# First expert's rows, w2 and the stores re-ordered at the handover from a recurrence to a mixture of experts

## Chip, cores and metric

One core of a Trainium2 chip runs the whole kernel as one launch. The metric is device microseconds. The time before is the median of three runs, 1148.8 us (1147.38 to 1150.54).

## What is computed

A gated linear recurrence over 4 sequences of 5056 steps and 256 channels, then a mixture of 8 experts over all 20224 rows, each row with one expert. Routing is greedy over the sorted logits, with a capacity of 2528 rows for each expert:

```python
f = lower_bound + (1 - lower_bound) * sigmoid(f_logit)
for t in range(S):
    h = f[:, t] * h + (1 - f[:, t]) * x[:, t]
    y[:, t] = h
logits = y.reshape(N, D) @ w_gate
# in descending order of all logits: token -> expert, unless taken or full
for e in range(E):
    hid = maximum(x[mask_e] @ w1[e], 0)
    out[mask_e] = hid @ w2[e]
```

## The kernel before, in words

**Stage one** goes over 40 chunks of four 128-row tiles (the last has two). For chunk i, `load` (L171) brings `f_logit` and `x` with two SyncE transfers, three chunks ahead, into pool `pin` (names `fl`, `xl`, four buffers each). `sig` (L843) is ScalarE's sigmoid and a product, on GpSimd for most chunks. `fwd` (L866) transposes both on TensorE (`pf`, `pb`), ScalarE makes the factor `fg`, VectorE scans to `g`. `back` (L896) multiplies `g` by identity and gate weights in fp32 (`iw`), which turns it back and adds the logits (`pr`, four PSUM buffers); ScalarE and VectorE copy this to `hr`, one slot of a ring of 22, and `store` (L921) writes it to `hbuf` in DRAM (528 KB). SyncE takes loads and stores in program order. The loop at L982 writes all this out by hand: iteration i does `fwd(i)`, `sig(i + 2)` and `back(i - 1)`; how many stores have been made by then is set by `SR` at L1010, and their order is `TURN` (L919).

**Beside stage one** a first, provisional expert is prepared from the first 72 tiles (18 chunks, `CE`): `prep` finds each row's best expert, `early` (L728) chooses the expert with the fewest rows above 896 and lists these rows, in jobs that ride along in `back`'s PSUM buffers. `first_weights(0..2)` (L964) bring its w1 in two halves of 0.5 MB and its w2 of 1 MB by indirect GpSimd transfers; `first_rows(q)` (L973) gathers its first four tiles of rows from `hbuf`, which needs the first 18 chunks stored. `low_half` (L978) makes the low parts of w1 (products are made of a high and a low fp32r part: `xh`, `xl`, `hh`, `hl`, `w1h`, `w1l`, and `w2s` with both).

**The handover** is at L1134: the remaining stores are issued, the stage-one pools are closed, and the pools of `moe` (L1146) are laid over the ring, so that the first writes into `hh`, `w2s` and others wait for the stores of the chunks that lay there.

**The experts**: slot -1 is the provisional expert's first 15 tiles, then come the slots 0 to 7. `trans` (L1323) turns gathered rows into `xh` and `xl`; `first` (L1342) makes six matmuls of 512 columns into `pw` (three PSUM buffers) for each of 8 blocks j, ScalarE makes `hh` and VectorE `hl` from it; `second` (L1372) multiplies by `w2s`, three steps behind (`LAG`). Everything else goes on between these: `tick` (L1551) gives steps to the routing (`main`), to the lists of rows (`comp`; `further` (L783) for slot -1) and to the split of weights (`sp`, `split`, L1233). Class `Pace` (L23) keeps an account of estimated engine times, and a step is emitted only if its engine is no more than 2 us ahead of TensorE in this account. Gathers of later rows are issued one per step, each held by the latest `hh`.

What stands at the handover in `moe`:

```python
XG[-1, 0] = g["XGE"].rearrange("p (q r) -> p q r", q=4)
asked[-1, 0] = 0
sp = Bg(split(-1))
trans(-1, 0, 0, True)
trans(-1, 0, 1, True)
g["low_half"](1)
for _ in range(2):
    sp.tick(True)
gather(*gathers.pop(0))
```

Of the kernel before, what the change touches and what calls it, by code (L numbers as in the profile page):

```python
# [7 lines left out]
F32 = mybir.dt.float32  # L8
F32R = mybir.dt.float32r
BF = mybir.dt.bfloat16  # L10
# [3 lines left out]
AF = mybir.ActivationFunctionType  # L14
# [92 lines left out]
def kernel(ctx: ExitStack, tc: tile.TileContext, x: bass.AP, f_logit: bass.AP,  # L107
# [9 lines left out]
    P = 128  # L117
# [16 lines left out]
    NX = NT + ND  # L134
    hbuf = dram.tile([N, ROW], F32, name="hbuf")
    ohp = ctx.enter_context(tc.tile_pool(name="ohp", bufs=2))
    ip = ctx.enter_context(tc.tile_pool(name="ip", bufs=E + 1))
# [9 lines left out]
    RING = 22  # L147
    SR = 0.5
    PS, RW, CP = 2, NT - CE, 136
# [4 lines left out]
    pre = ExitStack()  # L154
    pring = pre.enter_context(tc.tile_pool(name="pring", bufs=RING))
    pwork = pre.enter_context(tc.tile_pool(name="pwork", bufs=2))
# [9 lines left out]
    def rows_tile(dt):  # L166
        return pin.tile([P, KT * ROW], dt, name="fl")
# [171 lines left out]
    W = state.tile([P, NC], F32, name="W")  # L339
    MK = state.tile([P, NG, 16, 8], BF, name="MK")  # L340
    K16 = state.tile([P, NC], I16, name="K16")
# [386 lines left out]
    def early(wi, ids):  # L728
# [19 lines left out]
        yield  # L748
        first_weights(2)
        w = CE + 2  # L750
# [32 lines left out]
    def further(rt, ids, prog):  # L783

        cut(0, CE)
        yield 'DVE',
        for _ in prep(CP, NC):
            yield 'DVE',
        prog["all"] = True
        ranks(CE, NT)  # L790
        w = NT - CE + 2
        yield 'PE', RSE, ecnt
        ps = rt.tile([P, 512], F32, name="rt")
        offsets(ps, w)
        yield 'DVE', ps
        st = ohp.tile([P, len(groups)], F32, name="st")
        g1 = {}

        def ge(k):
            g1[k] = ohp.tile([P, 512], BF, name="g1")  # L800
            v.tensor_scalar(g1[k], IO, st[:, k:k + 1], None, op0=OP.is_ge)
        for k in range(2):
            v.tensor_scalar(st[:, k:k + 1], ps[:, 160:161], -512.0 * k, None, op0=OP.add)
        steps_of(ps, w, MORE)
        ge(0)
        at = EARLY // P
        for k, n in enumerate((4, MORE // P - 4)):
            yield 'PE', RAE, g1[k]
            ps = rt.tile([P, 512], F32, name="rt")
            for b in range(n):  # L810
                nc.tensor.matmul(ps[:, b * w:(b + 1) * w], g1[k][:, b * P:(b + 1) * P], RAE[:, :w], start=(b == 0),
                                 stop=(b == n - 1), skip_group_check=True)
            yield 'DVE', ps
            if k == 0:
                ge(1)
            yield from blocks(ps, 4 * k, n, w, CE * P, ids[:, at:at + n], True)
            at += n
            prog["ids"] = at
# [77 lines left out]
    def back(i, job=None):  # L896
        t0, n, _ = chunks[i]
        HR[i] = pring.tile([P, KT, ROW], F32, name="hr")
        for k in range(n):
# [18 lines left out]
    ST = {}  # L918
    TURN = [*range(18), 24, 18, 19, 20, 21, 23, 22, *range(25, NCH)]  # L919

# [47 lines left out]

    WSE, WSL, lows = [], [], []

    XGE = None

# [9 lines left out]
    for i in range(NCH + 1):  # L982
# [5 lines left out]
        if i < NCH:  # L988
            fwd(i)
        if i == NCH - 4:  # L990
            assert stored * KT >= CE
            XGE = rows_tile(F32R)
            first_rows(0)
        if i == 0:
# [3 lines left out]
        if i + 2 < NCH:  # L998
            sig(i + 2)
        if i == NCH - 4:  # L1000
            for q in range(1, KT):
                last_first = first_rows(q)
        if NCH - 2 <= i < NCH:
            WSE.append(pin.tile([P, FB, P], F32R, name="xl"))
            h = i - NCH + 2
            nc.scalar.activation(WSE[h][:, :4], RAWE[0][:, h].rearrange("p (q j) -> p j q", j=FB)[:, :4],
                                 AF.Identity, scale=omlb[:, h:h + 1])
        if i >= 1:
            back(i - 1, job)
            while stored < min(i - 1, int(SR * (i - 1)) + (i > 30)):  # L1010
                store(TURN[stored])
                stored += 1
        if i >= 4:
            build(2)
        if i > NCH - 2:
            h = i - NCH + 1
            WSL.append(pin.tile([P, FB, P], F32R, name="xl"))
            lows.append(h)
        upto = chunks[i - 1][0] // 8 * 8 if i else 0
# [3 lines left out]
        elif CE <= done < CP and upto >= done + 32:  # L1023
            preps.append(prep(done, done + 32))
            done += 32
        prep_step(99 if i == NCH else 3 if done == CE and upto < CE + 8 else PS if done < CE else (i != NCH - 4) + (i > NCH - 3))
        while lows and lows[0] == 0:
            low_half(lows.pop(0))
        if est is None and done >= CE and not preps:
# [89 lines left out]
    def afresh(rt):  # L1119
# [12 lines left out]
        ends(full)  # L1132

    for i in TURN[stored:]:  # L1134
        store(i)
# [10 lines left out]
def moe(ctx, tc, g):  # L1146
# [383 lines left out]
    prog[-1]["ids"] = EARLY // P  # L1530
    XG[-1, 0] = g["XGE"].rearrange("p (q r) -> p q r", q=4)
    asked[-1, 0] = 0
    sp = Bg(split(-1))
    trans(-1, 0, 0, True)
    trans(-1, 0, 1, True)
    g["low_half"](1)
    for _ in range(2):
# [13 lines left out]
    def tick():  # L1551
# [9 lines left out]
        if k < 0 and wn == 0 and sp is not None:  # L1561
            sp.tick(True)
            if sp.done:
# [155 lines left out]
```

## Time and profile before

| | |
|---|---|
| median of 3 runs | 1148.8 us |
| the profiled execution | 1148.47 us |
| its span (first to last instruction) | 1146.7 us |
| mean granted TensorE clock | 0.998 |
| TensorE busy | 1129.9 us, 99% |
| VectorE, ScalarE, GpSimd busy | 764.8, 542.1, 477.6 us |

Times in the rows are microseconds from the span's start. PE is TensorE's matmuls, PEld its weight loads, DVE VectorE, ACT ScalarE, POOL GpSimd, SPq SyncE's queue. Nearly all instructions are recorded through one helper, so they carry its line, L100, and are told apart by their tiles. In a timeline a row may merge several instructions (x4), and the bracket at its end is the idle time before it and what ended it. A matmul's end is modelled, so neighbouring rows overlap a little.

### The profile page before, as it was taken

The numbers are of one execution on the slowest core, as the hardware profiler recorded it, in microseconds if no ns is written. First come the engines' busy times: TensorE is split into PE (matmuls) and PEld (weight loads), VectorE is DVE, ScalarE is ACT, GpSimd is POOL, SyncE is SP. The second block draws the span as 40 slices with busy tenths as digits, with TensorE's granted clock in tenths as the row PEclk, the third lists the DMA queues.
The fourth block names the chain that finished last, engine by engine and source line by source line (L and its number), as shares of the span: only waits on it lengthen the run. The fifth ranks groups of instructions, "written<-read, shape, count | busy, mean of one in ns | idle before, by whom it ended". The sixth has DMA issues, their size and how long they took to land.

```text
span 1146.7 us, 21286 instructions
## 1 busy us (share of the span) xinstructions
PE 1129.9 (99%) x7905; PEld 1008.9 (88%) x7905; DVE 764.8 (67%) x2233; ACT 542.1 (47%) x1141; POOL 477.6 (42%) x486
## 2 busy tenths in 40 slices
PE   9999989999999999999999999999999999999997
PEld 7999879989888888888889888898889888888887
DVE  7999997778777446776875877656444643463342
ACT  7889873263337532643544444345434532242221
POOL 5777642243335663333433433343334333433322
PEclk9999999999999999999999999999999999999999
DMA  9999995131131111311311311131113111321100
GB/s 353 374 355 371 394 341 152 38 112 43 48 111 39 40 52 50 115 48 42 120 47 43 112 47 41 48 115 48 46 43 110 58 42 49 108 62 46 42 32 32
DMA packets 52947, 125.23 MB, mean 109 GB/s; under 512 B 8563, under 2 KB 28789, under 8 KB 51685
## 3 DMA queue, kind: packets, MB, share of 16 engines
q0 software_dynamic: 20016, 61.01, 16.5%
q1 hardware_dynamic: 32544, 62.78, 15.5%
q8 instruction: 64, 1.05, 0.4%
q14 instruction: 47, 0.38, 0.1%
q10 hardware_dynamic: 276, 0.01, 0.0%
HBM read 81.79 MB, written 42.10 MB: 108 GB/s over the span
## 4 chain that ended last, share of the span: by engine, by line
PE 91%; DMA 3%; DVE 2%; issue 1%; ACT 1%; POOL 1%; POOLq 0%; DVEq 0%; ACTq 0%; SPq 0%
PE pw L100 39%; PE py L100 35%; PE rt L100 7%; PE pr L100 5%; PE pb L100 2%; PE pf L100 2%; DVE g L100 1%; PE pt L100 1%; DMA fl<-in_f_logit_dram 1%; DMA hbuf<-hr 1%; DMA r<-in_moe_w_dram,wi 1%; DVE hl L100 0%; ACT fg L100 0%; POOL out_dram L100 0%; ACT hh L100 0%
## 5 line engine op out<-in xcount | busy, mean ns | idle before, releaser
L100 PE MATMUL py<-w2s,hh 128*128 128x256 f32 (+2 forms) x2120 | 434.4, 296 | 0.0
L100 ACT ACTIVATE hh<-pw 128x512 fp32r<-128x512 f32 (+3 forms) x328 | 190.8, 582 | 496.9 <-PE pw L100 439.7
L100 DVE SCALAR_TENSOR_TENSOR hl<-pw,hh 128x512 fp32r<-128x512 f32 (+3 forms) x328 | 219.3, 669 | 214.4 <-ACT hh L100 213.1
L100 PEld LDWEIGHTS py<-w2s,hh 128*128 128x128 f32 (+1 forms) x2120 | 341.9, 188 | 20.8 <-issue 0.2
L100 PE MATMUL py<-w2s,hl 128*128 128x256 f32 x1136 | 319.8, 282 | 0.0
L100 POOL DMA_INDIRECT out_dram<-y,ids x160 | 162.7, 1017 | 304.7 <-ACT hh L100 248.2
L100 POOL DMA_INDIRECT fl<-hbuf,ids x160 | 164.4, 1028 | 267.6 <-ACT hh L100 193.6
L100 PE MATMUL pw<-xh,xl 128*128 128x512 f32 (+3 forms) x672 | 231.6, 387 | 1.2 <-DVE hl L100 0.9
L100 PEld LDWEIGHTS py<-w2s,hl 128*128 128x128 f32 x1136 | 212.8, 187 | 2.0
L100 PEld LDWEIGHTS pw<-xh,xl 128*128 128x128 f32 x672 | 124.8, 189 | 19.5 <-DVE hl L100 1.3
L100 PE MATMUL pw<-xl 128*128 128x512 f32 (+3 forms) x336 | 130.5, 389 | 0.1
L100 PE MATMUL pw<-xl,w1h 128*128 128x512 f32 (+1 forms) x320 | 127.0, 397 | 0.0
L100 PE MATMUL pw<-xh,w1h 128*128 128x512 f32 (+1 forms) x320 | 126.3, 395 | 0.0
L100 PE MATMUL pw<-xh,w1l 128*128 128x512 f32 (+1 forms) x320 | 126.2, 394 | 0.0
L100 POOL TENSOR_TENSOR xl<-fl,xl 128x1024 f32<-128x1024 f32 x37 | 87.7, 2369 | 40.2 <-ACT fl L100 22.0
L100 DVE TENSOR_TENSOR_SCAN g<-fg,g,pb 128x512 f32<-128x512 f32 (+4 forms) x78 | 92.8, 1227 | 6.8 <-ACT fg L100 6.1
L100 PE MATMUL pr<-iw,g 128*128 128x136 f32 x632 | 81.1, 280 | 0.5 <-ACT hr L100 0.5
L100 ACT ACTIVATE junk<-rt,r 128x182 bf16<-128x182 f32 (+2 forms) x153 | 61.4, 402 | 37.3 <-DVE r L100 32.7
L100 PEld LDWEIGHTS pr<-iw,g 128*128 128x128 f32 x632 | 76.4, 190 | 1.0 <-ACT hr L100 0.9
L100 PEld LDWEIGHTS pw<-xh,w1l 128*128 128x128 f32 x320 | 60.2, 188 | 11.3
L100 PEld LDWEIGHTS pw<-xl 128*128 128x128 f32 x336 | 63.7, 190 | 5.9 <-DVE xl L100 0.5
L100 PEld LDWEIGHTS pw<-xh,w1h 128*128 128x128 f32 x320 | 60.4, 189 | 8.0
(271 smaller groups left out, 1537.6 us busy)
## 6 DMA issues: line engine op xcount, KB each, us to landing
hbuf<-hr SPq DMA_DIRECT2D x39, 528.0 KB, 9.9
fl<-in_f_logit_dram SPq DMA_DIRECT2D x38, 512.0 KB, 6.7
xl<-in_x_dram SPq DMA_DIRECT2D x38, 512.0 KB, 7.2
fl<-hbuf,ids POOLq DMA_INDIRECT x160, 2.8
out_dram<-y,ids POOLq DMA_INDIRECT x160, 2.4
fl<-in_f_logit_dram SPq DMA_DIRECT2D x3, 256.0 KB, 4.1
xl<-in_x_dram SPq DMA_DIRECT2D x3, 256.0 KB, 4.5
r<-in_moe_w_dram,wi POOLq DMA_INDIRECT x27, 5.3
```

What stands on the lines that cost most here:

```text
L100: r = f(*args, **kw)
```

## The change

The rows of the first expert are gathered into a buffer that shares its place with the routing masks (`mk`), in iterations 35 to 37 instead of 36. They are turned, in two of stage one's PSUM buffers, ahead of the last `back`, by `turn_first`, in place of the two calls of `trans`. `first_weights(2)` moves from `early` (about iteration 28) to iteration 37. The ring's slots get fixed names, laid out by `PLACE`, so that the pools of `moe` cover other chunks' slots. One store more is made from iteration 9, 17 and 25 on, 18 at most until iteration 37. The low half 0 comes right after `back(38)`, the low half 1 ahead of `back(39)`. In `further` the last `prep` comes ahead of `cut`. Slot -1's split of weights takes a step at every second tick.

```diff
+    mk = ctx.enter_context(tc.tile_pool(name="mk", bufs=1))
-    SR = 0.5
-    pring = pre.enter_context(tc.tile_pool(name="pring", bufs=RING))
+    pring = pre.enter_context(tc.tile_pool(name="pring", bufs=1))
+    PLACE = [2, 3, 4, 7, 8, 9, 6, 5, 18, 19, 20, 21, *range(10, 18), 0, 1]
+    for s in PLACE:
+        pring.tile([P, KT, ROW], F32, name=f"hr{s}")
-    MK = state.tile([P, NG, 16, 8], BF, name="MK")
+    XGE = mk.tile([P, NG * 64], F32R, name="MK")
@@ early
-        first_weights(2)
@@ further
+        for steps in (*preps, prep(CP, NC)):
+            for _ in steps:
+                yield 'DVE',
         cut(0, CE)
         yield 'DVE',
-        for _ in prep(CP, NC):
-            yield 'DVE',
@@ back
-        HR[i] = pring.tile([P, KT, ROW], F32, name="hr")
+        HR[i] = pring.tile([P, KT, ROW], F32, name=f"hr{i % RING}")
-    TURN = [*range(18), 24, 18, 19, 20, 21, 23, 22, *range(25, NCH)]
+    TURN = [*range(18), 18, 22, 19, 23, 20, 21, *range(24, NCH)]
+    MOST = CE // KT
+    def turn_first():
+        xs = [rows_tile(F32R)[:, :1024].rearrange("p (h w) -> p h w", h=2) for _ in range(2)]
+        pts = [ppr.tile([P, 512], F32R, name="pr") for _ in range(2)]
+        for h, pt in enumerate(pts):
+            for q in range(KT):
+                at = q * ROW + h * (P + E)
+                nc.tensor.transpose(pt[:, q * P:(q + 1) * P], XGE[:, at:at + P], ident_r)
+            nc.scalar.activation(xs[0][:, h], pt.bitcast(F32), AF.Copy)
+        for h, pt in enumerate(pts):
+            nc.vector.tensor_tensor(xs[1][:, h], pt.bitcast(F32), xs[0][:, h].bitcast(F32), op=OP.subtract)
+        return xs
@@ the loop over chunks
-        if i == NCH - 4:
-            assert stored * KT >= CE
-            XGE = rows_tile(F32R)
-            first_rows(0)
-        if i == NCH - 4:
-            for q in range(1, KT):
-                last_first = first_rows(q)
+        for q in {NCH - 5: (0,), NCH - 4: (1, 2), NCH - 3: (3,)}.get(i, ()):
+            assert stored >= MOST
+            last_first = first_rows(q)
+        if i == NCH - 3:
+            first_weights(2)
+        if i == NCH:
+            WSL.append(pin.tile([P, FB, P], F32R, name="xl"))
+            XSE = turn_first()
+            low_half(1)
         if i >= 1:
             back(i - 1, job)
-            while stored < min(i - 1, int(SR * (i - 1)) + (i > 30)):
+            while stored < min(i - 1, (i - 1) // 2 + (i > 8) + (i > 16) + (i > 24), MOST if i < NCH - 3 else i):
                 store(TURN[stored])
                 stored += 1
-        if i > NCH - 2:
-            h = i - NCH + 1
+        if i == NCH - 1:
             WSL.append(pin.tile([P, FB, P], F32R, name="xl"))
-            lows.append(h)
+            low_half(0)
-        prep_step(99 if i == NCH else ...)
-        while lows and lows[0] == 0:
-            low_half(lows.pop(0))
+        prep_step(0 if i == NCH else ...)
+    MK = mk.tile([P, NG, 16, 8], BF, name="MK")
@@ moe
-    XG[-1, 0] = g["XGE"].rearrange("p (q r) -> p q r", q=4)
-    asked[-1, 0] = 0
+    XS[-1, 0] = g["XSE"]
     sp = Bg(split(-1))
-    trans(-1, 0, 0, True)
-    trans(-1, 0, 1, True)
-    g["low_half"](1)
@@ tick
         if k < 0 and wn == 0 and sp is not None:
-            sp.tick(True)
+            if count[0] % 2:
+                sp.tick(True)
```

## Rows read from the trace of the kernel before

**Rows 1.** The page's first part, TensorE's entry of it.

```profile
PE 1129.9 (99%) x7905; PEld 1008.9 (88%) x7905; DVE 764.8 (67%) x2233; ACT 542.1 (47%) x1141; POOL 477.6 (42%) x486
```

**Rows 2.** Windows: length, busy us (instructions) by engine, granted clock, DMA share, GB/s.

```profile
20.00:40.00 20.00, 20.00 (x180) 20.00 (x179) 19.51 (x29) 17.98 (x31) 13.98 (x13) 1.00 1.04 393
120.00:140.00 20.00, 18.99 (x160) 17.79 (x160) 18.48 (x29) 17.82 (x35) 15.54 (x12) 1.00 1.05 392
159.00:165.00 6.00, 4.33 (x15) 2.86 (x15) 4.50 (x11) 4.48 (x7) 1.77 (x3) 0.73 1.07 357
165.00:171.00 6.00, 5.12 (x25) 4.02 (x24) 6.00 (x11) 3.46 (x7) 0.00 (x0) 0.98 1.10 341
240.00:400.00 160.00, 160.00 (x1207) 142.60 (x1206) 114.72 (x334) 79.59 (x206) 74.28 (x71) 1.00 0.19 57
```

**Rows 3.** Timeline of TensorE at the handover: start, us, instruction, idle before.

```profile
155.89 3.05 PE L100 MATMUL pr<-iw,g 128*128 128x136 f32 x24
...
160.09 0.28 PE L100 MATMUL pt<-identr,fl 128*128 128x128 f32 x1 [1.03 <-DMA fl<-hbuf,ids]
160.56 0.28 PE L100 MATMUL pt<-identr,fl 128*128 128x128 f32 x1 [0.19 <-DMA fl<-hbuf,ids]
...
161.53 0.61 PE L100 MATMUL pw<-xh,xl 128*128 128x512 f32 x1 [0.34 <-ACT xh L100]
...
168.67 0.50 PE L100 MATMUL pw<-xh,xl 128*128 128x512 f32 x1 [0.89 <-DVE hl L100]
```

**Rows 4.** The chain of waits, a group of six matmuls at full clock.

```profile
250.20 1.38 PE pw L100 x6
```

**Rows 5.** Timeline of VectorE around the handover.

```profile
150.33 1.48 DVE L100 TENSOR_TENSOR xl<-fl,xl 64x1024 f32<-64x1024 f32 x1
...
157.76 0.41 DVE L100 COPY hr<-pr 128x264 f32<-128x264 f32 x1
...
161.51 0.69 DVE L100 TENSOR_TENSOR xl<-pt,xh 128x512 fp32r<-128x512 f32 x1 [1.46 <-ACT xh L100]
...
162.72 1.14 DVE L100 SCALAR_TENSOR_TENSOR xl<-r,omlb,xl 128x512 fp32r<-128x512 f32 x1
...
167.91 0.70 DVE L100 SCALAR_TENSOR_TENSOR hl<-pw,hh 128x512 fp32r<-128x512 f32 x1
```

**Rows 6.** Timeline of GpSimd: the request of w2, then the first expert's gathers.

```profile
109.52 1.01 POOL L100 DMA_INDIRECT r<-in_moe_w_dram,wi  x1 [0.16 <-issue]
...
147.22 1.08 POOL L100 DMA_INDIRECT fl<-hbuf,ids  x1 [2.77 <-DMA hbuf<-hr]
...
150.88 1.85 POOL L100 DMA_INDIRECT fl<-hbuf,ids  x1 [0.16 <-PE pf L100]
...
154.34 0.99 POOL L100 DMA_INDIRECT fl<-hbuf,ids  x1 [0.30 <-issue]
```

**Rows 7.** Landing times: loads of 97 to 99, of 107 to 109, then w2's.

```profile
DMA to landing us min/median/max: 4.6/5.3/5.9
DMA to landing us min/median/max: 11.1/11.3/11.5
DMA to landing us min/median/max: 10.5/10.5/10.5
```

**Rows 8.** Timelines of ScalarE and VectorE behind the late load.

```profile
118.77 1.06 ACT L100 ACTIVATE fl<-fl 128x1024 f32<-128x1024 f32 x1 [2.56 <-DMA fl<-in_f_logit_dram]
121.37 2.45 DVE L100 TENSOR_TENSOR_SCAN g<-fg,g,pb 128x512 f32<-128x512 f32 x2 [1.92 <-ACT fg L100]
```

**Rows 9.** Timeline of SyncE's queue: a pair of stores, and the last stores.

```profile
120.36 1.55 SPq L923 DMA_DIRECT2D hbuf<-hr  x2
...
141.55 36.36 SPq L923 DMA_DIRECT2D hbuf<-hr  x22
```

**Rows 10.** Timelines of GpSimd and TensorE later on: a held gather, a gap.

```profile
186.25 1.02 POOL L100 DMA_INDIRECT fl<-hbuf,ids  x1 [25.47 <-ACT junk L100]
238.34 0.31 PE L100 MATMUL rt<-RA,g 128*128 128x160 bf16 x2 [1.95 <-DVE RA L100]
```

More of the change, by code (lines that the diff above doesn't have):

```diff
@@ L967, in first_weights @@
                                      in_offset=bass.IndirectOffsetOnAxis(ap=WIE[:, n:n + 1], axis=0))
-    WSE, WSL, lows = [], [], []
-    XGE = None
+    WSE, WSL = [], []
+    def turn_first():
[9 more added lines that the diff above has]
+        return xs
     def first_rows(q):
@@ L1025 @@
             done += 32
-        prep_step(99 if i == NCH else 3 if done == CE and upto < CE + 8 else PS if done < CE else (i != NCH - 4) + (i > NCH - 3))
-        while lows and lows[0] == 0:
-            low_half(lows.pop(0))
+        prep_step(0 if i == NCH else 3 if done == CE and upto < CE + 8 else PS if done < CE else (i != NCH - 4) + (i > NCH - 3))
         if est is None and done >= CE and not preps:
```

## Prediction

> **What bounds the kernel.** I read the page's busy shares first, then the windows, then the engines' own timelines around the point where the first stage hands over to the experts. TensorE is busy 1129.9 of 1146.7 us [rows 1], and from 240 us on it has no gap to give: 160.00 of 160.00 us at full clock [rows 2]. The change does not shorten that part, so whatever it wins or loses ahead of 240 us should arrive at the end almost unchanged.
>
> Two places ahead of 240 us hold lost time. One is the handover. The last product of stage one is 24 fp32 matmuls (with the chunk before it) from 155.89 on, 3.05 us, to 158.9. TensorE then waits 1.03 us for the third block of gathered rows, starts the first expert product at 161.53 and its fourth group only at 168.67, after 0.89 us of waiting for `hl` [rows 3]. At full clock a group of six takes 1.38 us [rows 4]; the three groups are 4.1 us, and the eight transposes about 0.5. So 168.67 - 158.9 - 4.6 = **5.2 us** are lost here. Part of it is clock: the mean granted clock of 159 to 165 is 0.73, so the engine ran some of that time on the 1.2 GHz level, after its waits [rows 2]. VectorE is the other half: it stands idle for 1.46 us until 161.51, waiting for the turned rows, and then has no gap (6.00 of 6.00 us from 165 to 171), with the first `hl` only at 167.91 [rows 2, 5].
>
> The other place is the last third of stage one. From 20 to 40 us TensorE loses nothing while 393 GB/s move; from 120 to 140 it runs 160 matmuls instead of 180, which at the earlier rate is 2.2 us lost, and VectorE is busy 18.48 [rows 2]. Loads issued at 97 to 99 us land after 5.3 us (the median of the row); those issued from 107 on, beside the first expert's weights, need 11.1 to 11.5 [rows 6, 7]. ScalarE waits 2.56 us for such a load at 118.77, and VectorE 1.92 us right behind it [rows 8].
>
> **The change part by part.** *Rows earlier.* The first gather stands at 147.22 after 2.77 us of waiting for a store, the fourth at 154.34 [rows 6], and the rows it brings are turned at 160.56, 6.2 us later [rows 3]. In the new order the first 18 chunks are stored by iteration 31 instead of 35, and the gathers are issued one iteration (3.6 us) earlier for the first, with the fourth at iteration 37. By POOL's order I put the fourth at about 151, so by the same 6.2 us, or one more under load, it lands at 157.2 to 158.2, just as the transposes can start (below). The buffer is the mask's; the masks come into use some 15 us after the transposes, so that wait costs nothing.
>
> *Turned ahead of the last product.* The transposes now stand in front of the last eight fp32 matmuls. They need the PSUM buffer that VectorE's copy of the chunk before frees at 158.1 [rows 5]. The two copies of the last chunk move 0.9 us back; the expert product's second PSUM bank waits for one of them. VectorE's idle 1.46 us is filled, and its order becomes: both `xl`, the low half, the last copies, then the product's needs.
>
> *Split at half the rate.* Before, VectorE ran six weight or routing steps ahead of the first `hl`. With one split step in two ticks, one 1.1 us half and one 0.6 us half of the weights move behind it. Today VectorE ends its copies at 160.05; without them, 0.6 us, it is free at 159.5. Counting its steps from there, by their lengths where they stand in [rows 5] and 0.25 us for each small routing step (an estimate from the timeline they fill between those rows): `xl` 1.2, low half 1.1, copies 0.6, three routing steps 0.75, a low half 1.2, another step 0.25, `hl` 0.6: the first `hl` ends near 165.2, and the fourth group can start some 3.4 us sooner than 168.67. But the second product needs the first low half of w2, which now comes behind another 1.2 us half and, if the planner lets the routing go first, 1.1 us of that: 167.2 to 168.3, against 170.2 before (168.67, a group, and the first matmul behind it). So the handover gives **2.0 to 3.0 us**; bounds 0 (rows late) and 3.4. I take 2.5, the middle of the inner pair, as both orders of the routing steps are open.
>
> *Weights for w2 later.* One megabyte leaves 109.52 [rows 6] for iteration 37. At 393 GB/s that is 2.7 us of transfers off the queue ahead of the late load. Against it stand three stores made sooner (1.4 us each at that rate), one of them at iteration 25, just before. So the late load comes 1.3 to 2.7 us sooner and ScalarE's 2.56 us shrink to about 1 or to nothing. TensorE gets back at most the 1.92 us of VectorE's wait, since VectorE is the bound afterwards; bounds 0 and 1.9, I take **1.2**, nearer the upper end because the pair of stores at 120.36 [rows 9], which follows the late load today, is gone as well. In its new place the transfer is queued on POOL for 1.0 us ahead of small copies that nobody needs for 5 us, and it lands beside the stores: issued at about 152, with 10.5 us as measured under load [rows 7], at 163, when ScalarE is ready for it. Cost 0 to 1 us, taken as 0: the slack is VectorE's, which needs its half at 166 or later.
>
> *Stores.* 22 stand behind the last load in both kernels (from 141.55 on [rows 9]). The end of the queue, which releases the third chunk's gather at 186.25 [rows 10], stays within 1 us of where it is: 2.7 us more for w2, less for the calmer queue ahead of it. The gather's product starts some 10 us later, so I cost this at nothing; without that cover it would be up to 3 us. The order of need matters where `hh` and `w2s` overwrite ring slots: those stores are the first six in either order, no wait shows before, and I count none.
>
> *Later.* The 1.95 us gap at 238.34 [rows 10] is caused by ScalarE's wait for the next weights in program order; the change does not touch it. The planner may shift it: 0 in the sum, 1.5 us either way in the range.
>
> **Sum.** Stage one 1.2 and handover 2.5 are 3.7 us. The profiled execution took 1148.47 us (span 1146.7, 1.8 around it), 0.3 under the median of 1148.8: 1148.5 - 3.7 = 1144.8, against the median 1145.1. I say **1145.0**, 0.33% under the median. About 0.3% (3.4 us) is what a measurement of this kernel can tell from no change, so this forecast lies on the edge.
>
> **A rule that speaks against it.** The gather issued at 150.88 took 1.85 us where the one at 154.34 took 0.99; VectorE's 64 x 1024 product of two SBUF tiles, from 150.33 on, ran beside the long one [rows 5, 6]. The fourth gather would move next to that product and could be 0.85 us later, on TensorE's path, since it is due within 1 us of its use; I leave that in the range. The Trainium skill, "SBUF — State Buffer", section "Who interferes with whom", says that a VectorE instruction with two SBUF inputs and a GpSimd instruction reading SBUF exclude each other for the whole instruction; the rows agree for this pair, and by the rule the sum would be 2.9 us rather than 3.7.
>
> On the shared transfers the row is the pair of loads that needed 11.1 to 11.5 us beside the weights [rows 7]. The Trainium skill, "DMA: Bandwidth & Descriptors", section "Issuing engines are not separate DMA queues", says that transfers of all queues run on the same 16 engines and interleave; by it w2 slows the last stores instead of the loads and nothing is saved in total, only placed where less waits.
>
> **The rivals.** *A, as above:* 1145.0, own range 1142.5 to 1146.0, chance 0.5.
> *B, the handover stays bound.* The fourth gather slips one iteration (3.6 us) or VectorE's queue takes the routing steps first. Then the transposes hold up the last product of stage one too, and what is left is VectorE's filled 1.46 us, or stage one's 1.2: 1147.0 to 1147.3. For it speaks that VectorE is the engine without slack on both sides of the handover; against it, that POOL is idle for 25 us later on and has room. It also covers a part that does not do what it says. Chance 0.38.
> *C, the early stores.* Stores doubled at iterations 9, 17 and 25 push loads past their need. A load that lands 2.56 us too late had needed up to 11.5 us, so the limit is about 8.9 [rows 7, 8]; the 20 us that begin with today's doubled store at 120.36 lost 2.2 us [rows 2, 9]. Three such places are 6.6 us; less 2.5 at the handover this gives 1148.5 + 4.1 = 1152.6. It decides from some 3.5 us of added landing time. Against it: a landing of 5.3 us ahead of the third place, and one store adds 1.4. Chance 0.12.
>
> So faster by over 0.3%: 0.5; within: 0.38; slower: 0.12. The range takes in the best case (1.9 + 3.4 = 5.3 us, and some from the gap at 238), and B with the planner's 1.5 us and w2's 1 us on the bad side: 1142 to 1150.5.
>
> **What would show it.** Right: no wait for gathered rows in front of the transposes; first expert matmul near 159.7 and fourth group near 165 to 166 on stage one's old clock; the granted clock of that stretch nearer 1; ScalarE's wait at 118.77 about 1 us or gone; no group of waits for loads near 45, 72 and 100 us. Wrong: a `w2s` or `hl` wait of over 2 us, a wait for the rows, a new wait near 199 us or 238 us that gives the time back.

## The result, and the profile after

The changed kernel is **slower**: 1155.94 us (median of six runs, 1154.61 to 1157.02) against 1150.61 us (1147.38 to 1151.33) for the kernel before, a ratio of 1.0055 (95%: 1.0046 to 1.0065). The forecast was 1145.0, with 1150.5 as the upper end. The profiled execution took 1154.61 us, span 1152.8; that of the kernel before 1148.47, span 1146.7. The 6.1 us between the spans are what has to be explained.

The page's first part, TensorE's and the others' busy time after, answers to [rows 1].

```profile
PE 1130.8 (98%) x7921; PEld 1013.5 (88%) x7921; DVE 763.7 (66%) x2231; ACT 541.7 (47%) x1142; POOL 477.9 (41%) x486
```

No engine has more to do: TensorE 0.9 us more, VectorE 1.1 less. The time is waiting, and the windows say where. After, with the columns of [rows 2] (length, busy us and instructions of PE, PEld, DVE, ACT, POOL, granted clock, DMA share, GB/s):

```profile
120.00:140.00 20.00, 19.39 (x172) 19.17 (x173) 19.47 (x34) 18.54 (x33) 15.51 (x12) 1.00 0.96 355
159.00:165.00 6.00, 5.07 (x24) 3.47 (x22) 5.83 (x13) 3.85 (x9) 2.72 (x3) 1.00 1.05 364
165.00:173.00 8.00, 6.17 (x26) 5.25 (x27) 7.85 (x18) 1.08 (x2) 0.00 (x0) 0.79 1.09 349
240.00:400.00 160.00, 160.00 (x1206) 142.68 (x1206) 113.80 (x330) 78.57 (x202) 75.24 (x72) 1.00 0.19 57
460.00:480.00 20.00, 16.71 (x100) 14.27 (x99) 12.19 (x41) 10.46 (x19) 6.88 (x7) 0.91 0.37 125
```

and two of these stretches in the kernel before:

```profile
165.00:173.00 8.00, 7.12 (x37) 5.57 (x35) 7.97 (x17) 3.46 (x7) 0.00 (x0) 0.99 1.10 340
460.00:480.00 20.00, 19.60 (x134) 17.51 (x133) 16.00 (x52) 12.90 (x24) 8.58 (x9) 1.00 0.42 138
```

The first two lines are what the prediction spoke of, and they gain. From 120 to 140 us TensorE runs 172 matmuls instead of 160. From 159 to 165 it is busy 5.07 us at clock 1.00, where it was busy 4.33 at 0.73. The third line gives that back (below). The last is a stretch the prediction never looked at: 2.9 us of busy time are missing there, and the clock is 0.91.

A way to see when a lead is lost is the start of ScalarE's k-th `hh` in its timeline, less the start of the same one in the profile of before (negative: ahead; us):

| | 1st (165) | 5th (173) | 9th (187) | 25th (237) | 29th (249) | 93rd (450) | 101st (475) | last (1137) |
|---|---|---|---|---|---|---|---|---|
| after | -3.31 | +0.09 | +0.06 | +0.14 | +1.72 | +1.36 | +5.83 | +6.14 |
| after, on a second chip | -4.06 | -0.66 | -0.68 | -0.34 | +1.17 | +0.85 | +3.53 | +3.52 |
| before, again | +0.37 | +0.29 | +0.26 | +0.51 | +0.42 | +0.53 | +0.60 | +0.61 |
| stores alone (below) | -1.07 | -1.13 | -1.13 | -0.94 | +0.45 | +0.39 | +0.51 | +0.52 |
| old list (below) | -2.48 | -1.37 | -0.05 | -0.04 | +1.42 | +1.43 | +1.81 | +1.87 |
| six memsets (below) | -3.58 | -0.15 | -0.19 | +2.06 | +4.05 | +3.72 | +3.75 | +3.97 |
| hold (below) | -3.38 | +0.01 | -0.04 | -2.73 | -2.07 | -1.66 | -2.34 | -2.92 |
| hold on before | +1.95 | +1.82 | +1.81 | -0.66 | +0.13 | -0.06 | -0.72 | -1.27 |

(Single executions, on three chips. Where the routing's matmuls fall between the products shifts a value too: the 23rd of after stands at +4.42, between +0.55 at the 21st and +0.14 at the 25th.) So three things happen: 3.3 us won are gone eight us later; 1.6 us go between 237 and 249 (0.8 of it is TensorE's idle time, 2.74 us from 230 to 242 against 1.95; the rest may be order alone, other matmuls that now fall between these products); 4.5 us go between 450 and 475 (2.7 in the execution on the second chip, the fastest of its five).

**The handover.** TensorE's timeline after, the answer to [rows 3], with two later gaps:

```profile
157.36 1.14 PE L100 MATMUL pr<-identr,MK 128*128 128x128 f32 x8
...
159.25 1.52 PE L100 MATMUL pw<-fl,xl 128*128 128x512 f32 x5
161.30 3.27 PE L100 MATMUL pw<-fl,xl 128*128 128x512 f32 x13 [0.52 <-DVE xl L100]
164.98 1.20 PE L100 MATMUL pw<-fl,xl 128*128 128x512 f32 x4 [0.41 <-DVE hl L100]
167.81 0.16 PE L100 MATMUL rt<-ecnt,tri 128*128 128x1 bf16 x1 [1.62 <-DVE EM L100]
...
169.20 0.63 PE L100 MATMUL py<-w2s,hh 128*128 128x256 f32 x2
...
234.80 0.23 PE L100 MATMUL rt<-RS,nsub 128*128 128x160 bf16 x1 [2.66 <-DVE RS L100]
...
474.78 0.37 PE L100 MATMUL rt<-RA,g 128*128 128x232 bf16 x2 [2.79 <-DVE to L100]
```

The eight transposes run as one row with no wait for the gathered rows, and the fourth group starts at 164.98 instead of 168.67. Then comes a wait that was not there: 1.62 us at 167.81 for the routing's `EM`. Behind it the matmuls take over half as long again (two of 256 columns 0.63 us at 169.20, 0.40 at 466.25). Counted as busy time multiplied by clock, TensorE does 5.1 instead of 3.2 us of work from 159 to 165, and 4.9 instead of 7.0 from 165 to 173: 1.9 won, 2.2 given back. VectorE, which it waits for (after):

```profile
164.25 0.68 DVE L100 SCALAR_TENSOR_TENSOR hl<-pw,hh 128x512 fp32r<-128x512 f32 x1
164.84 1.23 DVE L100 SCALAR_TENSOR_TENSOR xl<-r,omlb,xl 128x512 fp32r<-128x512 f32 x1
...
166.84 0.69 DVE L100 TENSOR_TENSOR w2s<-r,w2s 128x512 fp32r<-128x512 f32 x1
167.44 0.30 DVE L100 TENSOR_SCALAR_CACHE_REDUCE EM<-A,esc 128x86 f32<-128x86 f32 x1
```

It has no gap in this stretch. `EM` waits for no data; it stands last in a full queue.

**The weights at 460.** GpSimd after: the four gathers and w2 at the handover (two of the gathers shown), then the three requests for the next expert's weights, w1 in two halves and w2; all three rows carry the same names, so they do not tell which is which.

```profile
143.89 1.08 POOL L100 DMA_INDIRECT MK<-hbuf,ids  x1
...
151.25 1.02 POOL L100 DMA_INDIRECT MK<-hbuf,ids  x1 [0.16 <-issue]
152.57 0.97 POOL L100 DMA_INDIRECT r<-in_moe_w_dram,wi  x1 [0.30 <-DVE ids L100]
...
459.80 0.98 POOL L100 DMA_INDIRECT r<-in_moe_w_dram,wi  x1 [3.19 <-issue]
461.09 0.96 POOL L100 DMA_INDIRECT r<-in_moe_w_dram,wi  x1 [0.30 <-issue]
462.36 1.20 POOL L100 DMA_INDIRECT r<-in_moe_w_dram,wi  x1 [0.30 <-issue]
```

ScalarE after, which scales these weights into `w1h`, and, at its start, the late load of [rows 8]:

```profile
118.30 1.06 ACT L100 ACTIVATE fl<-fl 128x1024 f32<-128x1024 f32 x1 [0.87 <-DMA fl<-in_f_logit_dram]
...
463.98 1.28 ACT L100 ACTIVATE w1h<-r,omlb 128x512 fp32r<-128x512 f32 x1 [2.80 <-DMA r<-in_moe_w_dram,wi]
465.16 0.58 ACT L100 ACTIVATE hh<-pw 128x512 fp32r<-128x512 f32 x1
470.30 1.33 ACT L100 ACTIVATE w1h<-r,omlb 128x512 fp32r<-128x512 f32 x1 [4.56 <-DMA r<-in_moe_w_dram,wi]
```

and before:

```profile
465.68 1.29 ACT L100 ACTIVATE w1h<-r,omlb 128x512 fp32r<-128x512 f32 x1 [2.72 <-DMA r<-in_moe_w_dram,wi]
466.87 0.59 ACT L100 ACTIVATE hh<-pw 128x512 fp32r<-128x512 f32 x1
467.69 1.33 ACT L100 ACTIVATE w1h<-r,omlb 128x512 fp32r<-128x512 f32 x1 [0.22 <-DMA r<-in_moe_w_dram,wi]
```

Both wait for the first half by about the same. Only after does it wait 4.56 us for the second half, with the next `hh` behind it in program order, and TensorE runs dry behind that (2.79 us at 474.78). The packets tell why. The rows of w1 are moved as 4 KB packets, those of w2 as 8 KB. After, from 462 to 463, from 464 to 466 and from 467 to 469 us:

```profile
DMA packets 80, 0.33 MB, mean 328 GB/s; under 512 B 0, under 2 KB 0, under 8 KB 80
DMA packets 79, 0.60 MB, mean 299 GB/s; under 512 B 4, under 2 KB 4, under 8 KB 8
DMA packets 162, 0.60 MB, mean 299 GB/s; under 512 B 30, under 2 KB 30, under 8 KB 148
```

and before, from 464 to 466 and from 468 to 470:

```profile
DMA packets 164, 0.61 MB, mean 303 GB/s; under 512 B 16, under 2 KB 16, under 8 KB 164
DMA packets 68, 0.56 MB, mean 279 GB/s; under 512 B 0, under 2 KB 0, under 8 KB 0
```

After, 4 KB packets are followed by 8 KB packets (71 of 79) and these by 4 KB packets again; before, the 8 KB packets come last. So after, **w2 is asked for second, at 461.09, and w1's second half third, at 462.36**. The time from request to landing of the second request, first after, then before, says the same:

```profile
r<-in_moe_w_dram,wi POOLq DMA_INDIRECT x1, 7.8
r<-in_moe_w_dram,wi POOLq DMA_INDIRECT x1, 4.8
```

Before, it lands at 467.66 and ScalarE starts on the second half at 467.69. After, it lands at 468.91, and ScalarE waits on until 470.30: the semaphore that it waits for there is that of the third request, and that of the second is waited for by ScalarE's copy of w2 at 481.9.

The source lists w1, w1, w2 in both kernels. But the schedule that is kept by hand around `moe` names TensorE, VectorE and ScalarE only; GpSimd's order is left to the framework, and beside the changed order of the others it comes out with the two requests exchanged. So w1's second half is asked for behind w2's 1 MB and used 7.9 us after its request, where it landed after 4.8 before. The same bytes move; the half needed first lands last.

### The profile page after: what moved, and what is told of

Read it like the earlier page. It is cut to its first block, busy times and chain, and to the rows that moved or that the text cites. A ratio compares the mean times of both kernels' runs of the same rounds, so it can differ in the third digit from the quotient of the medians.

```text
span 1152.8 us, 21324 instructions
## 1 busy us (share of the span) xinstructions
PE 1130.8 (98%) x7921; PEld 1013.5 (88%) x7921; DVE 763.7 (66%) x2231; ACT 541.7 (47%) x1142; POOL 477.9 (41%) x486
## 4 chain that ended last, share of the span: by engine, by line
PE 76%; DVE 1%; issue 1%; DMA 1%; ACT 0%; POOL 0%; POOLq 0%; ACTq 0%
PE pw L100 36%; PE py L100 33%; PE rt L100 7%; PE pt L100 1%; DMA r<-in_moe_w_dram,wi 1%; DVE hl L100 0%; ACT hh L100 0%; POOL out_dram L100 0%; DVE y L100 0%; POOLq L1726 0%; DVE w1l L100 0%; DVE g L100 0%; DVE GP L100 0%; DVE RA L100 0%; DVE sc L100 0%
## 5 line engine op out<-in xcount | busy, mean ns | idle before, releaser
L100 PE MATMUL py<-w2s,hh 128*128 128x256 f32 (+2 forms) x2144 | 440.8, 297 | 0.0
L100 PEld LDWEIGHTS py<-w2s,hh 128*128 128x128 f32 (+1 forms) x2144 | 347.8, 189 | 24.0 <-issue 2.7
L100 POOL DMA_INDIRECT fl<-hbuf,ids x156 | 157.8, 1011 | 262.3 <-ACT hh L100 195.5
L100 PE MATMUL pw<-xh,xl 128*128 128x512 f32 (+3 forms) x640 | 219.7, 385 | 0.0
L100 PEld LDWEIGHTS py<-w2s,hl 128*128 128x128 f32 x1144 | 215.4, 188 | 1.7
L100 PEld LDWEIGHTS pw<-xh,xl 128*128 128x128 f32 x640 | 118.7, 189 | 17.0 <-issue 0.5
L100 PE MATMUL pw<-xl 128*128 128x512 f32 (+3 forms) x320 | 123.7, 387 | 0.0
L100 PEld LDWEIGHTS pw<-xl,w1h 128*128 128x128 f32 x320 | 60.2, 188 | 6.2
```

Of the source, the lines that this page charges most:

```text
L100: r = f(*args, **kw)
```

## The experiments

Every ratio is against the kernel before, run on the same chip in turn. There are two kinds of chip among them: on the first the kernel before takes about 1149.7 us, on the second, three chips, 1158.3 to 1159.4, and there VectorE and ScalarE show late starts with nothing waited for (last section). Ratios are compared within a chip.

**First: is it the weights' split that comes too early?** The changed kernel once more; the split of each later expert held for 24 ticks, in the changed kernel and in the kernel before; and slot -1's split at its old rate.

```diff
 a_later, b_later (split; tick)
+        begun[k] = count[0]
+        if k > 0:
+            yield 'ACT',
-        elif not sp.done:
+        elif not sp.done and (k < 0 or "left" in prog[k + 1] or count[0] >= begun.get(k + 1, 0) + 24):
 a_fullrate (tick)
-            if count[0] % 2:
-                sp.tick(True)
+            sp.tick(True)
```

> The changed kernel once more, unaltered. Theory one (the loss is a fixed property of the new order of instructions: ScalarE reaches its first two pieces of the next expert's weights while they are still on the way, near 464 and 470 us): 1154.6 to 1157, ScalarE's wait for the second half of w1 again 4 us or more near 466 to 470, TensorE's gap 2.5 us or more behind it. Rival one (that landing of 9.2 us was an accident of the one profiled execution): the same total, but the wait under 1 us, and the lost time somewhere else.

> The changed kernel, with the first piece of each expert's weight split held back until 24 planner ticks (about 10 us) after the request. Theory one: ScalarE's waits for weights go (2.8 and 4.6 us near 460 to 470, 5.6 near 230), TensorE's gaps behind them go with them (2.8 us at 474.78, part of 2.7 at 234.80), and the clock keeps its level at 475 to 480: 1146 to 1150. Rival two (the loss is made by the new order of the handover, and the late weights only show where it surfaces): 1153 or more, with the gap at another place.

> The kernel before, with the same hold of 24 ticks. Theory one: its own gap at 238.34 (1.95 us) and ScalarE's 4.5 us wait for weights before it shrink, the rest stays: 1146 to 1150, and a_later is 1 to 2 us below it, the part of the change that works. Rival two: no change, 1149 to 1151, and a_later over it.

> The changed kernel with the first expert's remaining weight split at every tick, as before, in place of every second one. Theory one: the handover loses up to 1 us, and everything behind it is emitted in another order, so that the wait near 470 may be there or not: anything from 1147 to 1157. Rival three (the slower split is what costs): 1148 to 1150, with the second product of the first expert earlier than 169.20.

Measured, on a chip of the second kind (before 1159.38): a_again 1160.27 in one run; a_later 1.0029 (1.0016 to 1.0041); b_later 1.0040 (1.0026 to 1.0055); a_fullrate 0.9996 (0.9979 to 1.0013). With the hold of 24 ticks both kernels are slower than the kernel before. Why is not shown: the longest new wait of a_later's TensorE, 2.32 us at 423.71, goes back to ScalarE standing idle for 4.64 us until 422.15, and what ended that the profile does not tell. So this hold says nothing of the theory. In a_again w2 is asked for second too, and the second half is waited for (3.61 us at 476.98). In a_fullrate w1's second half is asked for second, and TensorE has no such wait.

**Second: the parts.** The kernel before again; the changed kernel on another chip; the changed kernel with w2's request meant to go out later; and, on the kernel before, the stores' order and the ring's slots alone.

```diff
 a_r2late (split)
-        issue(upto=lambda what: what == ("w", k))
+        if k >= 0 and issues[:1] and issues[0][0] == ("w", k):
+            issue(2)
 ...
+            if k >= 0 and i == 4:
+                issue(upto=lambda what: what == ("w", k))
 b_stores (kernel before)
+    PLACE = [2, 3, 4, 7, 8, 9, 6, 5, 18, 19, 20, 21, *range(10, 18), 0, 1]
-    TURN = [*range(18), 24, 18, 19, 20, 21, 23, 22, *range(25, NCH)]
+    TURN = [*range(18), 18, 22, 19, 23, 20, 21, *range(24, NCH)]
-            while stored < min(i - 1, int(SR * (i - 1)) + (i > 30)):
+            while stored < min(i - 1, (i - 1) // 2 + (i > 8) + (i > 16) + (i > 24), MOST if i < NCH - 3 else i):
```

> The kernel before, unaltered, for a profile from the same chip as the others of this call. The last four kernels ran on a chip where before took 1159.4 us, 9 us more than in the pair the result stands on, and there VectorE and ScalarE show starts at 360 to 440 us that wait for nothing (0.7 to 5 us each). If that is a property of the chip, it is in this profile too and the time is near 1159; if it belongs to the edits, it is not, and the time is near 1150.

> The changed kernel, unaltered, timed against before in five rounds. If the loss of 0.55% is the order of the change alone: ratio 1.004 to 1.007 on any chip. If it hangs on how fast a chip brings weights and instructions: a ratio that differs from 1.0055 by more than 0.002 wherever before itself is not at 1150, 0.998 to 1.003 at 1159.

> The changed kernel; of each next expert's three weight requests the third (w2, 1 MB) goes out at a later step, so that the two halves of w1 have the queue to themselves. Theory one with the sharing of the queue as its cause: the second half of w1 lands in under 6 us near 460 to 480 (9.2 before), ScalarE's second wait there falls under 1 us, and the total is 2 to 5 us below the changed kernel on this chip. If the late half is not made by w2's transfer: its landing stays over 8 us, total within 1.5 us of the changed kernel.

> The kernel before with the stores and ring slots of the change alone. Its part of the forecast: chunk 40 starts 1.2 us earlier (153.1 in place of 154.3), bounds 0 to 1.9. If that gain reaches the end: ratio 0.998 to 0.9995. If what follows the handover swallows it or turns it into a loss, as in the whole change (3.3 us ahead at the first expert's first product, 0.1 behind at its fifth): ratio 1.000 to 1.006, with chunk 40 early all the same.

Measured (before 1149.57): b_again 1149.08 in one run; a_again2 1.0051 (1.0037 to 1.0065), so the loss is there on a second chip; a_r2late 1.0057 (1.0041 to 1.0072); b_stores 0.9992 (0.9982 to 1.0002). The edit of a_r2late did not do what it was meant to: written later in the source, w2's request still goes out second (460.79) and w1's second half third (462.05, landing after 7.4 us just as ScalarE starts on it at 469.51). So it is a third run of the changed kernel and no test. The stores alone are worth nothing measurable. Their last chunk comes 0.15 us earlier than in b_again, not 1.2. Their first product is 1.4 us ahead of b_again's, and that is lost at 238 us. Windows of b_stores there, then of b_again:

```profile
238.00:242.00 4.00, 4.00 (x18) 3.68 (x17) 3.10 (x7) 2.60 (x6) 0.15 (x1) 0.57 0.00 0
```

```profile
238.00:242.00 4.00, 3.26 (x21) 2.95 (x22) 3.97 (x10) 3.15 (x8) 0.00 (x0) 1.00 0.03 14
```

The gap ahead of it is the same wait for `RA` in both (1.94 and 2.10 us). In b_stores the clock is then mostly on the 1.2 GHz level, and 18 matmuls fit where otherwise 21 do in less busy time; in b_again it stays at 1.00.

**Third: the old list of rows, the order of the requests, the hold.** a_drain gives the changed kernel the old order of the routing steps back. a_gap writes six small memsets for GpSimd between the request of w1's second half and w2's, and changes nothing else in the source. a_hold and b_hold hold the first split piece of every expert for 14 ticks.

```diff
 a_drain (further; the loop over chunks)
-        for steps in (*preps, prep(CP, NC)):
-            for _ in steps:
-                yield 'DVE',
         cut(0, CE)
         yield 'DVE',
+        for _ in prep(CP, NC):
+            yield 'DVE',
-        prep_step(0 if i == NCH else ...)
+        prep_step(99 if i == NCH else ...)
 a_gap (the issues of an expert's weights)
+                      (("w", k), lambda: [nc.gpsimd.memset(gap, 0.0) for _ in range(6)][-1]),
 a_hold, b_hold (as a_later, with k >= 0)
-        elif not sp.done:
+        elif not sp.done and ("left" in prog[k + 1] or count[0] >= begun.get(k + 1, 0) + 14):
```

> The changed kernel with VectorE's mask preparation drained ahead of the transposes again and the cut first in the first expert's further list, as before. In the changed kernel TensorE waits 1.6 us at 167.05 to 167.8 for VectorE's EM, and the clock then shows its lower level until 171.5. If that wait is the order of the further list: it is gone, the second product starts by 167 (169.20 changed, 170.18 before), and the clock stays up; total 1 to 3 us below the changed kernel, unless the waits near 235 and 470 take it back. If VectorE is merely full there: a wait as long for xl or hl instead, within 0.5 us of the changed kernel at the second product.

> The changed kernel with six small GpSimd memsets between the request for the second half of w1 and that for w2, about 0.5 to 1 us; the order of every other instruction is the same. In the changed kernel w2's 8 KB packets run ahead of the 4 KB packets of the second half of w1 at 463 to 467, and w2's request takes 1.20 us there against 0.95 elsewhere. If that overtaking hangs on what VectorE does at that moment, it goes: the second half lands within 6 us, ScalarE's second wait near 470 is under 1 us (3.4 to 4.6 changed), and the total is 2 to 4.5 us lower, ratio 1.001 to 1.003. If the overtaking belongs to the place in the queue: it stays, and so does the ratio of 1.005.

> The changed kernel with the first piece of every expert's split, that of the second expert at 230 included, held back 14 planner ticks (about 5 us) behind the request. If ScalarE's waits for weights make the gaps at 235 (2.7 us) and 470 (1.6 to 2.8): both go, 1147 to 1151, ratio 0.998 to 1.001. If the planner's new order puts other waits in their place, as the hold of 24 ticks seemed to do: ratio 1.003 or more.

> The kernel before with the same hold. If ScalarE's wait at 230 to 234 (4.5 us) makes the gap at 238.34 (1.95 us): it goes, and the time is 1 to 2.5 us under before, ratio 0.998 to 0.999. If the order only moves: 0.999 to 1.004.

Measured (before 1149.76): a_drain 1149.35, 0.9987 (0.9978 to 0.9997); a_gap 1152.08, 1.0019 (1.0010 to 1.0029); a_hold 1145.79, 0.9964 (0.9950 to 0.9978); b_hold 1145.63, 0.9959 (0.9945 to 0.9973).

The texts above that speak of w2 overtaking w1's second half in the queue read the rows of GpSimd by the source's order; it is the requests that stand in another order.

*a_gap* is the cleanest test of the 4.5 us: in the traces TensorE, VectorE and ScalarE run the same instructions in the same order as after, from start to end, and GpSimd alone differs. GpSimd, the landing of its second request, ScalarE and the window in a_gap:

```profile
463.46 0.96 POOL L100 DMA_INDIRECT r<-in_moe_w_dram,wi  x1 [0.30 <-issue]
464.40 0.21 POOL L100 MEMSET gap<- 128x96 f32 x1
464.78 1.15 POOL L100 DMA_INDIRECT r<-in_moe_w_dram,wi  x1 [0.17 <-issue]
```

```profile
r<-in_moe_w_dram,wi POOLq DMA_INDIRECT x1, 5.0
```

```profile
466.32 1.28 ACT L100 ACTIVATE w1h<-r,omlb 128x512 fp32r<-128x512 f32 x1 [2.78 <-DMA r<-in_moe_w_dram,wi]
467.50 0.58 ACT L100 ACTIVATE hh<-pw 128x512 fp32r<-128x512 f32 x1
468.46 1.32 ACT L100 ACTIVATE w1h<-r,omlb 128x512 fp32r<-128x512 f32 x1 [0.38 <-DMA r<-in_moe_w_dram,wi]
```

```profile
460.00:480.00 20.00, 19.52 (x136) 17.32 (x135) 15.28 (x53) 12.59 (x24) 8.88 (x14) 1.00 0.37 132
```

Only one of the six memsets runs between the requests; the other five come at 469.37. But the order of the requests is the old one again: the second, at 463.46, lands after 5.0 us, at 468.44, and ScalarE starts on the second half at 468.46. The 4.56 us wait is 0.38, and the table's row gains nothing and loses nothing at 475 (+3.72, +3.75). By the ratios this is worth 0.0032 of 1150 us, 3.7 us, against a_again2 on another chip of the same kind. What remains of a_gap's loss is at 237 to 249, where its clock is 0.50 from 234 to 240.

*a_hold* and *b_hold* both ask for w2 second (b_hold too, where the kernel before does not), but ScalarE comes to the second half when it is there. ScalarE and the window in a_hold:

```profile
468.38 1.26 ACT L100 ACTIVATE w1h<-r,omlb 128x512 fp32r<-128x512 f32 x1
...
470.96 1.28 ACT L100 ACTIVATE w1h<-r,omlb 128x512 fp32r<-128x512 f32 x1
```

```profile
460.00:480.00 20.00, 20.00 (x139) 17.88 (x138) 13.35 (x45) 13.15 (x29) 7.89 (x9) 1.00 0.42 133
```

No wait before the weights, 20.00 of 20.00 us busy, and from 230 to 250 us TensorE has no gap either. Both kernels come to the same time, 0.4% under the kernel before: with the late weights out of the way **the whole change is worth nothing that five runs of each can tell** (1145.15 to 1146.83 against 1145.38 to 1147.21).

*a_drain* takes the other side away. TensorE's timeline in it:

```profile
166.70 0.28 PE L100 MATMUL py<-w2s,hh 128*128 128x256 f32 x1
...
168.68 0.16 PE L100 MATMUL rt<-ecnt,tri 128*128 128x1 bf16 x1 [0.57 <-DVE EM L100]
...
174.50 0.33 PE L100 MATMUL rt<-RAE,g 128*128 128x88 bf16 x4 [1.66 <-DVE g L100]
```

The second product starts at 166.70, the wait for `EM` shrinks to 0.57 and the clock of 165 to 171 stays at 1.00. But the wait comes back as 1.66 us for `g`, and by the ninth `hh` the lead is zero here too. Its small gain over the kernel before comes with the requests at 460 in their old order.

**Fourth and fifth: again, on two more chips of the second kind** (before 1158.83 and 1158.31). a_drain_hold joins a_drain and the hold; the others are the kernels above.

> The changed kernel with the split at every tick, again. If the loss comes from the two new orders together (half rate and further list), undoing either one takes it away: w1's second half lands ahead of w2 again near 462 to 475, ratio 0.998 to 1.001. If the further list alone is the cause: the overtaking and the ratio of 1.005 stay. The first expert's second product later than in a_drain (166.70) by the wait for hl, up to 2 us.

> The changed kernel with the hold of 14 ticks, again, beside b_hold2 on one chip. If the gain forecast for stage one (1.2 us) reaches the end once the weights are no longer waited for: 1 to 2 us below b_hold2. If the handover's own waits (EM 1.6 us, lower clock behind it) keep eating it: within 0.7 us of b_hold2.

> The kernel before with the hold of 14 ticks, again: ratio 0.9945 to 0.9975 as in b_hold, 3 to 4.5 us under before.

> The changed kernel with the old order of the further list and the hold of 14 ticks. If the two causes are apart and add up: the EM wait goes at the handover (second product by 167) and ScalarE's waits go at 230 and 470, 1 to 2.5 us below a_hold2 and b_hold2, ratio 0.994 to 0.996. If whatever is ahead at 173 is used up by 187, as the first experts' products show in every variant so far: within 0.7 us of b_hold2.

> The changed kernel with the split at every tick, once more. Where before takes 1150 us: 0.998 to 1.001 if the loss comes from the two new orders together, 1.004 to 1.007 if from the further list alone; gaps of its own at 199 (rows, 1.8 us) and 245 (2.6 us) as on the other chips. Where before takes 1159: 0.999 to 1.001, which tells nothing new.

> The changed kernel with the old order of the further list and the hold of 14 ticks. Where before takes 1150 us, b_hold took 1145.6 and a_hold 1145.8: 1143 to 1145, ratio 0.9935 to 0.996, if the two add up; 1145 to 1147 if not. Where before takes 1159: 0.996 to 0.998 as just now.

Measured: a_fullrate2 1.0004 (0.9989 to 1.0020) and a_fullrate3 1.0016 (1.0002 to 1.0030); a_hold2 0.9985 (0.9969 to 1.0001), b_hold2 0.9988 (0.9977 to 1.0000); a_drain_hold 0.9970 (0.9958 to 0.9982), a_drain_hold2 0.9972 (0.9957 to 0.9987). Changed and unchanged kernel are alike under the hold again. On these chips the hold is worth less, and the old list with the hold is the best of those tried: on the chip where both ran, a_drain_hold took 1155.11 and b_hold2 1157.07. So there, with the new list undone, some 2 us of the rest of the change seem to reach the end; a_drain_hold2 ran without b_hold beside it. The three profiles of full rate have the requests in their old order. Full rate ran on chips of this kind alone, where the unaltered change was run once, so whether it alone takes the whole loss away stays open.

The best versions are the kernel before or the changed kernel with the hold of 14 ticks (1145.63 and 1145.79), some 4 us under the kernel before on its chip and better than both.

## Why the prediction was wrong, step by step

**The step that failed** is the prediction's first argument: from 240 us on TensorE "has no gap to give", so "whatever it wins or loses ahead of 240 us should arrive at the end almost unchanged". It was read off one window of 160 us, and it holds inside that window after the change too (160.00 of 160.00). But the kernel goes on for 750 us. The order of the instructions depends on what stood before it, in the new order w2 is asked for ahead of w1's second half, and at 470 us ScalarE waits 4.56 us in front of `hh`. TensorE's missing 2.9 us in 460 to 480 and the clock of 0.91 over 20 us (at most 1.8 us) are together 4.7, the table's 4.5. a_gap takes this away by itself and a_hold does it another way; of all steps this one is shown best. The prediction put "1.5 us either way" on the planner and looked for it at 199 and 238 us alone. From 3.7 us won to 6.1 us lost are 9.8 us: 3.7 are the forecast gain, which is gone at the fifth `hh`, 1.6 go around 240 us and 4.5 at 470.

**Stage one, 1.2 us:** right. The last chunk's first transpose starts at 153.07 instead of 154.30, and at 152.22 on the second chip. ScalarE's wait of 2.56 us for the late load is 0.87 at 118.30, with 1.84 at a load before it. The reason given, that w2's move does it and the stores add little, fits b_stores, which won 0.15 here; w2's move alone wasn't run.

**Rows earlier, turned first:** right. The gathers run at 143.89 to 152.27; TensorE waits for none here; in most other executions of the new order it waits for one, 0.19 to 0.62 us. The first expert matmul is at 159.25 where 159.7 was said, the fourth group at 164.98 where 165 to 166 was said, and the first `hl` ends at 164.93 where 165.2 was said. (Not six weight or routing steps stood ahead of the first `hl` before, but eight behind the low half: three of the split and five of the routing.)

**Handover, 2.5 us:** the lead is real at the first product (3.3) and gone by the fifth. The working stopped at the second product, and even there it missed: 167.2 to 168.3 was said "if the planner lets the routing go first", 169.20 came, because `EM` is a wait on TensorE and not only a step on VectorE, and because the clock fell behind it. The prediction counted VectorE's steps up to `hl` and took what TensorE gains as kept. But those steps are moved, not removed: VectorE is busy 5.83 and 7.85 us in 159 to 165 and 165 to 173, against 4.50 and 7.97. The rival *B* ("the handover stays bound", "VectorE's queue takes the routing steps first") described this. a_hold against b_hold gives its size, as far as two orders can be compared: nothing measurable is left, where B kept 1.2 to 1.5 us. The half rate of the split has its part in this. At full rate `EM` is not waited for, and in all three profiles a lead is still there at the ninth `hh` (2.1, 1.8 and 4.7 us; a_again, on the chip of the first of them, is 0.1 behind there). It goes later, in each of them in part on a wait of 1.8 to 2.0 us for gathered rows, here in a_fullrate3:

```profile
197.01 0.28 PE L100 MATMUL pt<-identr,fl 128*128 128x128 f32 x1 [1.87 <-DMA fl<-hbuf,ids]
```

That is the place near 199 us that the prediction named as a sign of being wrong.

**w2's new place, stores, stores' need:** costed at nothing, and TensorE's timeline shows no wait for w2 at the handover, and the gather that the last stores release is at 186.57 instead of 186.25. Rival *C*, early stores, did not happen: the matmuls of 120 to 140 us went up.

**"Later", 0 with 1.5 either way:** 1.6 us between the 25th and 29th `hh`, so its bad end was met, if only half of it by idle time. The wait at 238.34 has become one of 2.66 us at 234.80. The clock doesn't fall there after the change (1.00 from 234 to 242), but it does in b_stores, a_drain (0.69 from 238 to 242) and a_gap.

**The rule on SBUF** (2.9 instead of 3.7) decided nothing: all four gathers took 1.00 to 1.08 us, none the 1.85 of [rows 6].

## What to carry to other kernels

Where a planner orders instructions, a local gain is only a new starting point for it: look for every place later on where an in-order engine waits for a transfer with little slack, and cost the chance that the order tips there. An order that a wait depends on should be held, and read from the trace: requests of one name are told apart by their packets and by who waits for their landing, not by the source. (A fixed order of the three requests was not tried.) Such a place is best mended by itself; here a hold on the split of weights gives 0.4% on one kind of chip, and 0.1% at the edge of noise on the other, with or without the change. And follow a lead past the first product: steps moved on the engine that bounds a stretch come back a few microseconds later.

## What the runs showed of the hardware

**Requests on one queue, served in their order.** The three requests are on one queue and some 1.3 us apart. After (4 KB, 8 KB and 4 KB rows) and before (4 KB, 4 KB and 8 KB rows) their packets come in the order of the requests, with some overlap. The Trainium skill, "DMA: Bandwidth & Descriptors", section "Two DMAs through the same engine are not ordered", says that descriptors of one queue of one engine start in order while nothing orders transfers across engines. For whole requests these rows agree with the first half; single engines were not looked at. What w2's 1 MB ahead costs the half of 0.5 MB behind it: 7.9 us from request to use, against 4.8. In 11 of the 20 profiles the third request of this expert takes GpSimd 1.20 to 1.21 us, against 0.93 to 0.97 in the others (1.15 in a_gap), and these 11 are the ones with w2 asked for second; why it takes longer there is open.

**The same gap, two clocks.** After gaps of 1.94 and 2.10 us before the same matmul the clock was 0.57 and 1.00 in the next stretch. No row here tells which it will be. It cost b_stores 1.4 us between its 25th and 29th `hh`, and a_gap 1.9 us ahead of its 25th, against after.

**Chips differ.** On three of the chips VectorE and ScalarE start some instructions late with nothing waited for, most of them between 360 and 440 us, as VectorE in a_again:

```profile
407.88 0.69 DVE L100 SCALAR_TENSOR_TENSOR hl<-pw,hh 128x512 fp32r<-128x512 f32 x1 [2.59 <-issue]
```

The same kernel takes some 9 us longer there. Why was not tried.
